# Weight preparation and two heads in a written-out order on every engine, in a Conformer block's forward and backward kernel

## The chip, the cores and the metric

The kernel runs on one core of one Trainium2 chip. The metric is the device time of one execution in microseconds (us); lower is better. Kernels are compared only within the same rounds. A profiled execution also gives a trace with every instruction's start and duration. "Span" is its time from the first to the last instruction.

The engines are called as in the profile: PE is TensorE's matmul, PEld its weight load, DVE is VectorE, ACT is ScalarE, POOL is GpSimd, SP is SyncE, which issues DMAs here. SPq and ACTq are the DMA issues of SP and of ACT.

## The reference

Two batches of 4000 tokens, 144 channels, bfloat16. One layer norm feeds an attention of one head and a gated convolution path; the reference returns the output and the gradients of `x` and all seven weights.

```python
xa  = _layernorm(x)
q, k, v = split(xa @ w_qkv)
p   = softmax(q @ k.T * D ** -0.5)                 # 4000 x 4000 per batch
glob = (p @ v) @ w_att_out
u, g = split(gelu(xa @ w_mlp_in))
gc  = depthwise_conv(_layernorm(g), dw_csgu)       # 5 taps
loc = (u * gc) @ w_mlp_out
m   = concat(glob, loc)
out = x + (m + depthwise_conv(m, dw_merge)) @ w_merge
# returned: out and the vjp for grad_out with respect to x and the 7 weights
```

## The kernel before

The program works on batch 0 and then batch 1, each in three stages: a **head**, the **attention** (32 row blocks of scores, forward and backward at once) and a **tail**. Only the heads are changed. A head turns `x` and `grad_out` into what the attention needs, in eight groups of 512 tokens. Its parts for a group g:

- normalisation (batch 0 alone; batch 1's is done earlier): `stats` on DVE, `power` on POOL, `nm` on DVE, then `apply`, shared among ACT, DVE and POOL;
- `stT` transposes the normalised `x` on PE, with copies out of PSUM on ACT and DVE;
- `stA` transposes `grad_out`; its last 16 channels are first packed for five taps by a POOL instruction (the group "g" in the profile, "narrow" below), and the copies out go to ACT and DVE;
- `stB(n)` multiplies, for two blocks of 128 tokens at a time: `pq` (the scores' left side Q) and `pb` (the gradient with the taps folded into the weights, in `GL`), and copies them out to `Q_t` and `B_t` on ACT and to `dug` on DVE. The head does the first eight of sixteen such steps; the rest run inside the attention.

Batch 0's head also prepares the weights: `M1` (the product of the q and k weights), the tap-scaled products `GL`, and others that are needed only later. `Weights.first` stands ahead of the groups, `Weights.second` behind them. A list scheduler orders the instructions on each engine from the program; the programmer's order is a priority, not an order of execution.

```python
def turn(self, src, R, c0, C, name, ps, pool=None):      # a weight, transposed
    ...
    if C % 128:
        nc.vector.memset(t[:, nck - 1, :], 0.0)
    for cc in range(nck):
        for kt in range(nk):
            ...
            pt = ps.tile([128, 128], BF, tag="tp", name="pt")
            nc.tensor.transpose(pt[0:w, 0:rk], src[...], self.W.ident[0:rk, 0:rk])
            nc.vector.tensor_copy(t[0:w, cc, kt * 128:kt * 128 + rk], pt[0:w, 0:rk])

def first(self, ps, then):
    ... # loads, then() = loads of x and of grad_out's first three groups, transposes, M1
    for h in range(2):
        ...
        for kt in range(2):
            for kk in range(5):
                if h == 0:
                    nc.vector.tensor_scalar(A[:, kt, 4 - kk, :], UT[h][:, kt, :], W.wm[:, h, kt, kk:kk + 1], None, op0=ALU.mult)
                else:
                    nc.gpsimd.tensor_scalar(A[:, kt, 4 - kk, :], UT[h][:, kt, :], W.wm[:, h, kt, kk:kk + 1], 1.0, op0=ALU.mult, op1=ALU.mult)
                nc.gpsimd.tensor_scalar(Bz[:, kt, 4 - kk, :], Wmh[:, h, kt, 128:D], W.wm[:, h, kt, kk:kk + 1], 1.0, op0=ALU.mult, op1=ALU.mult)
        ... # products of Wmh with A and of Bz with UT into GL, GL80

def apply(self, g):
    nc.vector.scalar_tensor_tensor(nm[:], mv[:, :, 0], -1.0, rs, op0=ALU.mult, op1=ALU.mult)
    for j in range(4):
        if self.b or j % 2 == 0:
            nc.scalar.activation(self.S.xaa[:, g * 4 + j, :], xg[:, j, :], ACT.Identity, bias=nm[:, j:j + 1], scale=rs[:, j:j + 1])
        else:
            (nc.vector if j == 1 else nc.gpsimd).tensor_scalar(...)

# phase_head:
for s in range(NGR + 2):
    if s < NGR:
        stA(s)                       # in batch 0 with stats, power, apply of group s
    if 0 <= s - 1 < NGR:
        stT(s - 1)
    if s == NGR:                     # 16 rows of R into the attention's operand
        nc.sync.dma_start(S.R_d[:], R[112:128, :])
        ... # 8 copies (batch 1) or 4 (batch 0), "row copies" below
    if 0 <= s - 2 < NGR:
        stB(s - 2, ...)
    if s == 5:
        ... # QB, jt0: the operand of the first score row
if wts:
    wts.second(ps_t, ps_2)
```

## Time and profile before

| | before |
|---|---|
| time, three runs | 1294.88 us (1293.71 to 1295.97) |
| span of the profiled execution | 1288.0 us (this execution's time was 1289.89 us, some 5 us under the median of these three) |
| first `pb` of batch 0 | 32.25 us |
| first score matmul (`pS`) of batch 0 / of batch 1 | 63.74 / 680.18 us |
| first `y` (second product of the attention) of batch 0 / of batch 1 | 95.91 / 708.97 us |

The page of the profile, parts 1 and 4: busy time (share of the span) and number of instructions of each engine, then how the chain of work that ended last divides among the engines.

```profile
PE 1211.8 (94%) x15116; PEld 949.9 (74%) x15116; DVE 962.3 (75%) x3293; ACT 843.5 (65%) x2498; POOL 558.8 (43%) x1033
...
PE 71%; DVE 13%; DMA 4%; issue 4%; ACT 4%; POOL 3%; SPq 1%; ACTq 0%; DVEq 0%; POOLq 0%
```

PE is busy for 94% of the span, so most of the kernel is bound by matmuls; but these are the attention and the tails. The heads look different. The next table gives the busy time of each engine in stretches of 3 us of before's head of batch 0 (columns: stretch, its length, then busy us and instructions of PE, PEld, DVE, ACT and POOL, the granted clock of PE, the share of DMA, GB/s; before's trace has no record of the clock ahead of 31.57 us, and the view prints 1.00 there).

```profile
19.00:22.00 3.00, 1.02 (x3) 0.28 (x3) 1.76 (x10) 0.89 (x2) 3.00 (x10) 1.00 0.68 240
22.00:25.00 3.00, 0.00 (x0) 0.00 (x0) 0.00 (x0) 0.00 (x0) 3.00 (x12) 1.00 0.00 0
25.00:28.00 3.00, 0.43 (x4) 0.44 (x5) 0.00 (x0) 0.00 (x0) 3.00 (x12) 1.00 0.00 0
28.00:31.00 3.00, 2.87 (x17) 1.96 (x16) 1.78 (x8) 1.06 (x3) 1.00 (x7) 1.00 0.71 246
```

From 22 to 28 us POOL works almost alone. The chain of waits of before names the work (columns: start, us, what):

```profile
26.83 0.25 POOL w_Bz L1224
27.08 0.44 POOL g L1428
27.57 0.65 PE pr L1431 x4
```

It is the end of a run of 30 small tap-scaled copies on POOL (ten of `w_A` and twenty of `w_Bz`, begun at 18.06 us; ten more of `w_A` are on DVE), then the packing of `grad_out`, then PE. The view of waits sums, from 9 to 60 us, the idle time of each engine by the instruction that waited and the one that released it (columns: who waited <- for whom: us in total, times, longest).

```profile
DVE nm L1383 <- POOL rstdx L1376: 9.6, 7, 4.0
...
DVE w_GL L1230 <- PE fw L1229: 8.5, 2, 8.0
...
PE pr L1431 <- POOL g L1428: 8.4, 3, 7.0
ACT ra L1386 <- DVE nm L1383: 8.3, 8, 4.3
```

PE and DVE wait for POOL and its results. Once `GL` stands, before's eight steps of `stB` in the head follow within 24.1 us (the first `pq` at 32.0 us, the eighth at 56.1).

### The profile page before, as it was taken

The numbers are of one execution on the slowest core, as the hardware profiler recorded it, in microseconds if no ns is written. First come the engines' busy times: TensorE is split into PE (matmuls) and PEld (weight loads), VectorE is DVE, ScalarE is ACT, GpSimd is POOL, SyncE is SP. The second block draws the span as 40 slices with busy tenths as digits, with TensorE's granted clock in tenths as the row PEclk, the third lists the DMA queues.
The fourth block names the chain that finished last, engine by engine and source line by source line (L and its number), as shares of the span: only waits on it lengthen the run. The fifth ranks groups of instructions, "written<-read, shape, count | busy, mean of one in ns | idle before, by whom it ended". The sixth has DMA issues, their size and how long they took to land.

```text
span 1288.0 us, 39900 instructions
## 1 busy us (share of the span) xinstructions
PE 1211.8 (94%) x15116; PEld 949.9 (74%) x15116; DVE 962.3 (75%) x3293; ACT 843.5 (65%) x2498; POOL 558.8 (43%) x1033
## 2 busy tenths in 40 slices
PE   4899999999999999998989999999999999998996
PEld 2657777777777777788975777777777777778994
DVE  4656778888888788857735677888878878885674
ACT  2667777767767766546646767777777767664542
POOL 6412444545444453257611244444544445324650
PEclk9999999999999999999999999999999999999998
DMA  6378989898989989887775889899888999987861
GB/s 185 88 142 147 156 155 159 155 167 151 161 151 159 170 155 165 151 190 216 202 220 109 152 156 152 153 169 170 148 160 153 154 170 155 164 154 182 238 168 29
DMA packets 634223, 205.51 MB, mean 160 GB/s; under 512 B 577183, under 2 KB 631556, under 8 KB 633988
## 3 DMA queue, kind: packets, MB, share of 16 engines
q1 hardware_dynamic: 627472, 197.54, 80.6%
q10 hardware_dynamic: 6548, 5.33, 1.7%
q8 instruction: 120, 1.97, 0.6%
q14 instruction: 83, 0.68, 0.2%
HBM read 46.22 MB, written 21.79 MB: 53 GB/s over the span
## 4 chain that ended last, share of the span: by engine, by line
PE 71%; DVE 13%; DMA 4%; issue 4%; ACT 4%; POOL 3%; SPq 1%; ACTq 0%; DVEq 0%; POOLq 0%
PE y L1911 15%; PE pS L1865 9%; PE X L1933 9%; PE X L1934 8%; PE pD L1865 7%; PE pS L1861 5%; DVE Sm L1875 5%; PE pc L1573 3%; PE pb L1467 2%; PE po L2088 2%; PE EF L2063 1%; DVE jg L1792 1%; PE gr L2159 1%; DVE acc L1949 1%; ACT Qs L1894 1%
## 5 line engine op out<-in xcount | busy, mean ns | idle before, releaser
L1875 DVE SCALAR_TENSOR_TENSOR Sm<-pD,Pm 128x500 bf16<-128x500 f32 x512 | 325.7, 673 | 80.3 <-PE pD L1865 47.6
L1873 ACT ACTIVATE Pm<-pS 128x500 bf16<-128x500 f32 x512 | 295.5, 586 | 41.2 <-PE pS L1865 38.3
L1933 PE MATMUL X<-Qs,Sm 128*128 128x144 bf16 x2048 | 285.6, 226 | 9.3 <-DVE acc L1949 8.9
L1946 POOL TENSOR_TENSOR acc<-xs,acc 128x432 f32<-128x432 f32 x150 | 168.5, 1123 | 280.5 <-ACT xs L1945 280.0
L1934 PE MATMUL X<-Bt,Pm 128*128 128x144 bf16 x2048 | 285.4, 226 | 0.7 <-DVE Bt L1898 0.7
L1934 PEld LDWEIGHTS <-Pm 128*128 128x128 bf16 x2048 | 199.9, 98 | 11.9 <-issue 11.3
L1933 PEld LDWEIGHTS <-Sm 128*128 128x128 bf16 x2048 | 199.8, 98 | 1.5 <-issue 0.9
L1911 PEld LDWEIGHTS <-PT 128*128 128x128 bf16 x2048 | 136.5, 97 | 30.7 <-issue 2.4
L1911 PEld LDWEIGHTS <-ST 128*128 128x128 bf16 x2048 | 136.4, 97 | 27.6
L1945 ACT COPY xs<-X 128x432 f32<-128x432 f32 x150 | 77.9, 519 | 111.4 <-PE X L1934 103.4
L1949 DVE TENSOR_TENSOR acc<-X,acc 128x432 f32<-128x432 f32 x180 | 104.0, 578 | 53.9 <-PE X L1934 53.2
L1873 ACT ACTIVATION_READ_ACCUMULATOR Pm<-pS 128x1 f32 x512 | 105.0, 205 | 0.0
L1861 PE MATMUL pD<-rb,QBr 16*128 16x500 bf16 x448 | 96.0, 378 | 3.3 <-DVE Sm L1875 2.8
L1865 PEld LDWEIGHTS <-BTm 128*128 128x128 bf16 x512 | 49.8, 98 | 59.9 <-issue 1.6
L1861 PE MATMUL pS<-rb,QBr 16*128 16x500 bf16 x448 | 91.9, 380 | 0.1
L1792 DVE SCALAR_TENSOR_TENSOR jg<-gnC,dgC 128x256 bf16<-128x256 bf16 x160 | 89.6, 560 | 1.0
L1921 POOL TENSOR_TENSOR B_t<-zd,yd 128x144 bf16<-128x144 f32 x64 | 34.0, 531 | 113.0 <-ACT zd L1920 112.7
L1865 PEld LDWEIGHTS <-QTm 128*128 128x128 bf16 x512 | 29.1, 97 | 72.5 <-issue 72.5
L1865 PE MATMUL pS<-rb,QTm 128*128 128x500 bf16 x256 | 76.9, 382 | 0.0
L1865 PE MATMUL pS<-ra,QTm 128*128 128x500 bf16 x256 | 76.5, 381 | 0.0
L1911 PE MATMUL y<-rb,PT 128*128 128x144 bf16 x1024 | 74.3, 226 | 1.0 <-ACT zd L1920 1.0
L1911 PE MATMUL y<-ra,PT 128*128 128x144 bf16 x1024 | 74.3, 226 | 1.1 <-ACT zd L1920 1.1
(626 smaller groups left out, 2895.0 us busy)
## 6 DMA issues: line engine op xcount, KB each, us to landing
gs<-in_grad_out_dram SPq DMA_DIRECT2D x24, 720.0 KB
dh_d<-dh SPq DMA_DIRECT2D x32, 144.0 KB
dhr<-dh_d SPq DMA_DIRECT2D x16, 288.0 KB
gs<-in_grad_out_dram SPq DMA_DIRECT2D x8, 540.0 KB
xg<-in_x_dram SPq DMA_DIRECT2D x21, 144.0 KB
dug_d<-dug SPq DMA_DIRECT2D x16, 144.0 KB
dug<-dug_d SPq DMA_DIRECT2D x32, 72.0 KB
ug_d<-ug SPq DMA_DIRECT2D x32, 72.0 KB
```

What stands on the lines that cost most here:

```text
L1573: nc.tensor.matmul(pc[:, q, 0:128], t[:, q * 128 + m:q * 128 + m + 128], W.dg[:, (4 - m) if back else m, :], start=(m == 0), stop=(m == 4))
L1792: nc.vector.scalar_tensor_tensor(jg[:], a_[:, m:m + 256], 1.0, d_[:, 2:258], op0=ALU.mult, op1=ALU.mult, accum_out=dws[:, p, m:m + 1])
L1861: nc.tensor.matmul(o_[h][:, 0:SC], jt[i // 4][2][rr, i % 4, :], S.XR[c2][rr, 0:SC], start=True, stop=False)
L1865: nc.tensor.matmul(o_[h][:, 0:SC], jt[i // 4][w][:, i % 4, :], S.xaT[:, c0:c0 + SC], start=False, stop=True)
L1873: nc.scalar.activation(P[:, pb, c1:c1 + SC], o_[h][:, 0:SC], ACT.Exp, accum_out=ld8[:, 0, n_:n_ + 1])
L1875: nc.vector.scalar_tensor_tensor(Sm[:, pb, c1:c1 + SC], o_[h][:, 0:SC], 1.0, P[:, pb, c1:c1 + SC], op0=ALU.mult, op1=ALU.mult, accum_out=l ...
L1911: nc.tensor.matmul(y[:, w, :], src[:, jj, :], S.xaa[:, j, :], start=(j == 0), stop=(j == NBK - 1))
L1933: nc.tensor.matmul(X[:, jj, :], Sm[:, i % NP, j * 128:(j + 1) * 128], Qs[:, i % 4, :], start=(kk == 0 and jj == 0), stop=False, skip_group ...
L1934: nc.tensor.matmul(X[:, jj, :], P[:, i % NP, j * 128:(j + 1) * 128], Bt[:, i % 4, :], start=False, stop=(kk == 1), skip_group_check=True)
L1945: nc.scalar.copy(xs[:, 0:nj, :], X[:, 0:nj, :])
L1946: nc.gpsimd.tensor_tensor(a_, xs[:, 0:nj, :], a_, op=ALU.add)
L1949: nc.vector.tensor_tensor(a_, X[:, 0:nj, :], a_, op=ALU.add)
```

## The change

The intent: prepare the weights earlier and with fewer instructions, share the work among DVE, POOL and ACT, and write out by hand the order of every engine, so that weight work that is needed later fills the gaps between the groups rather than stand behind them. In particular:

1. transposes of one weight share one PSUM bank and two copies; the zero fills of the transposed weights go to POOL;
2. the 40 scaled copies (30 on POOL, 10 on DVE) become four 720-wide products (two on DVE, two on POOL) and four 80-wide ones on DVE;
3. `second` becomes a generator `rest`, of which one portion runs after each group; `G` takes three copies per half; its weight stores go to ACT's queue; `apply` of both odd blocks of a group (j = 1 and 3) goes to POOL;
4. both heads stand in a `manual_schedule` block: each engine executes its instructions in exactly the order of the program.

The core of the diff:

```diff
 def turn(...):
         if C % 128:
-            nc.vector.memset(t[:, nck - 1, :], 0.0)
+            nc.gpsimd.memset(t[:, nck - 1, :], 0.0)
+        pt = ps.tile([128, nck, R], BF, tag="tp", name="pt")
         for cc in range(nck):
             for kt in range(nk):
-                pt = ps.tile([128, 128], BF, tag="tp", name="pt")
-                nc.tensor.transpose(pt[0:w, 0:rk], ...)
-                nc.vector.tensor_copy(t[0:w, cc, kt * 128:kt * 128 + rk], pt[0:w, 0:rk])
+                nc.tensor.transpose(pt[0:w, cc, kt * 128:kt * 128 + rk], ...)
+        n1 = C // 128
+        nc.vector.tensor_copy(t[:, 0:n1, :], pt[:, 0:n1, :])
+        if C % 128:
+            nc.vector.tensor_copy(t[0:C % 128, n1, :], pt[0:C % 128, n1, :])
 ... (40 copies out)
+    def taps(self):
+        for kt in range(2):
+            nc.vector.tensor_tensor(self.A[0][:, kt], self.UT[0][:, kt, :].unsqueeze(1).to_broadcast([128, 5, D]),
+                                    self.wr[:, 0, kt, :].unsqueeze(2).to_broadcast([128, 5, D]), op=ALU.mult)
+        ... # four products Bz, 80 wide, on DVE
+    def taps1(self, kt):
+        self.k.nc.gpsimd.tensor_tensor(self.A[1][:, kt], ...)          # 720 wide
 ... (second -> rest, with yields; memsets, dg, c80, WIM copies to gpsimd)
-            nc.sync.dma_start(W.fin[name][0][:], t[:])
+            nc.scalar.dma_start(W.fin[name][0][:], t[:])
 ... (apply)
-                (nc.vector if j == 1 else nc.gpsimd).tensor_scalar(...)
+                nc.gpsimd.tensor_scalar(...)
 ... (phase_head)
-        for s in range(NGR + 2):
-            ...
-        if wts:
-            wts.second(ps_t, ps_2)
+        with tc.manual_schedule():
+            ...
+            if wts:
+                wts.heads(ps_t, ps_2)
+                nrm.stats(0)
+                nrm.power(0)
+                wts.taps()
+                wts.taps1(0)
+                nrm.apply(0)
+                narrow(0)
+                wts.taps1(1)
+                wts.keys(ps_t, ps_2)           # w_qT, w_kT and M1
+                nrm.stats(1)
+                ...
+                rest = wts.rest(ps_t, ps_2)
+            ...
+            for n in range(-1, NGR):
+                if wts and 0 <= n + 4 < NGR and n >= -1:
+                    nrm.stats(n + 4)
+                    nrm.power(n + 4)
+                if 2 <= n + 3 < NGR:
+                    if wts:
+                        nrm.apply(n + 3)
+                    narrow(n + 3)
+                if n >= 0:
+                    stB(n, *tiles())
+                if 1 <= n + 2 < NGR:
+                    stT(n + 2)
+                    stA(n + 2)
+                    ...
+                if n == 5:
+                    spread()                   # R_d and all row copies
+                if n == 3:
+                    jit()
+                if rest:
+                    next(rest, None)
```

## The prediction

> **What bounds it now.** The span is 1288.0 us (timed median 1294.88), PE busy 94%. The chain of waits is 71% PE, nearly all in attention and tails, which the change leaves alone. Only the two heads change. Batch 0's first score matmul (pS) starts at 63.8 us and its first y group at 96.1; batch 1's at 680.3 and 709.1. Batch 1's head needs no weights and takes 24.4 us from the release of its buffers (655.9); so of batch 0's 64 us roughly 9 are first loads, 24 head, 30 weights and waits.
>
> The chain of the first 70 us names these waits: PE's second group of transposes waits for grad_out until 9.3 us, with weight work queued behind it. From 18.1 to 27.1 GpSimd makes 30 small scaled copies (w_Bz 293 ns, w_A 381 ns); in the stretches 22-25 and 25-28 the others are almost idle. Then each group passes the GpSimd power (1.01 us) and DVE. From 58 to 65 weight leftovers run, and the granted clock is about 0.5 from 62.5 to 69.
>
> **What the change does.**
> 1. Weight products come ahead of grad_out: PE and DVE can work from about 3 us. Gain 4 us.
> 2. The 30 copies become two 720-wide GpSimd products and DVE products. From GpSimd's two-input products (531 ns at 144 wide, 800 at 288, 1123 at 432) I estimate 1.7 us each: 3.5 us for 9.3. Gain 6 us.
> 3. Transposes share one bank and two copies instead of four; G takes three copies per half instead of six: some 40 fewer DVE/ACT instructions of 0.15-0.3 us. Leftovers are spread between groups, so most of 58-65 vanishes. Gain 3-5 us.
> 4. Costs: GpSimd takes memsets, diagonals, WIM copies and all odd normalisations, in order: the second product stands behind the narrowing of grad_out, the w_q/w_k memsets behind that. Adding up its list with the trace's durations, M1 is ready about 15 us, first pb about 20 (now 32.3), and the eighth narrowing ends about 43. Seven zero stores (0.45 us of issue each) move ahead of part of the first grad_out load. Cost about 3 us.
>
> So first pS comes at about 50 us, and GpSimd, not PE, paces batch 0's head. [...]
>
> Batch 1: same operations; PE paces it (2.8 us a group, about 2.6 of it matmul issue). The row copies into the attention operand now all issue after the last transposed group, where some went earlier. Gain 0-2 us.
>
> Clock: [...] the trace shows 0.50 at 64-68. Without the leftovers there, another 1-2 us.
>
> **Sum.** 14 (batch 0) + 1 (batch 1) + 1 (clock) = 16 us, all on the critical path, since attention cannot start earlier: **1279 us, range 1269 to 1288** (8 in 10). Faster by over 2%: 0.11; within 2%: 0.87; slower: 0.02.
>
> **What would show it.** First pS of batch 0 at 45-55 us, first pb near 20; no stretch over 3 us with GpSimd alone busy; GpSimd nearly full from 12 to 43. Batch 1 from release to first pS in 23-25 us. Attention and tails unchanged to 2 us.
>
> **What would make it wrong.** GpSimd slower than estimated, so that the order blocks PE behind it; grad_out landing late behind tiny loads on the queue; half clock through the head; batch 1's scores waiting for row copies. Or all waits go and pS comes near 40: over 20 us saved.

The 1-2 us for the clock are the estimate from the 0.50 in before's trace; that the clock would rise without the leftovers was not shown.

## The result and the profile after

Ratios here and below are the mean time of one kernel's fast runs over the mean of the other's fast runs of the same rounds, so they are not quite the ratio of the medians quoted beside them. Values below 1 mean faster than before.

| | before | after |
|---|---|---|
| time, median of four runs each | 1294.3 us (1291.9 to 1295.97) | 1296.85 us (1295.13 to 1298.43) |
| ratio to before, 95% interval | | 1.0021 (1.0000 to 1.0042) |
| span of the profiled execution | 1288.0 us | 1294.6 us |
| first `pb` of batch 0 | 32.25 us | 26.43 us |
| first `pS` of batch 0 / of batch 1 | 63.74 / 680.18 us | 66.83 / 682.58 us |
| first `y` of batch 0 / of batch 1 | 95.91 / 708.97 us | 96.81 / 713.51 us |

The predicted 1279 us (1269 to 1288) was missed: no gain showed, in place of 16 us. Of the 6.6 us between the two spans, some 4 are before's lucky execution; the timed medians differ by 2.6 us.

```profile
PE 1212.3 (94%) x15116; PEld 951.6 (74%) x15116; DVE 957.4 (74%) x3236; ACT 843.4 (65%) x2494; POOL 562.3 (43%) x1032
...
PE 71%; DVE 13%; DMA 4%; issue 4%; ACT 4%; POOL 1%; SPq 1%; ACTq 0%; DVEq 0%; POOLq 0%
```

PE's busy time is the same to 0.5 us. In the chain, POOL's share fell from 3% to 1%, so the 30 copies did leave it, but the span did not shrink with it.

Where the difference arises can be read from the attention. Its 32 rows in each batch start with one ACT instruction each; in after it starts 0.9 us later than in before in every row of batch 0, and 4.5 us later in every row of batch 1. Each attention therefore takes the same time, 463.0 us from its first such instruction to its last in both kernels. Of the 6.6 us between the spans, 0.9 arise ahead of batch 0's rows and 3.6 between the two batches' rows, where batch 0's tail and batch 1's head lie. The last 2.1 us lie behind the last row: the last tail took 130.1 us in after and 128.1 in before. No run changes the tail, and over the fourteen profiles it took 127.8 to 132.2 us, so these 2.1 us are within its spread. What counts is the chain ahead of the first row of each batch.

**Batch 0.** The first `pb` comes 5.8 us earlier, the first `pS` 3.1 us later. In between, after's eight steps of `stB` take 39.1 us (`pq` from 25.9 to 65.0 us) where before took 24.1. The view of waits of after, for the same stretch:

```profile
ACT ra L1415 <- DVE nm L1412: 12.0, 5, 5.6
...
PE fw L1151 <- DVE w_kT L1141: 8.1, 1, 8.1
PE tp L1457 <- ACT rb L1466: 7.6, 3, 3.3
POOL ve L1404 <- DVE nm L1412: 6.9, 4, 3.1
...
DVE go80f L1460 <- PE tp L1457: 5.0, 4, 2.2
...
ACT ra L1415 <- DMA wf_U<-w_l_s: 3.3, 1, 3.3
```

Now every engine waits for another: ACT for DVE, PE for ACT and DVE, DVE for PE, POOL for DVE. Here are six single microseconds of after (columns as in the stretches above):

```profile
34.00:35.00 1.00, 0.96 (x11) 0.59 (x9) 0.65 (x4) 0.00 (x0) 0.47 (x3) 1.00 0.89 318
35.00:36.00 1.00, 0.41 (x5) 0.31 (x5) 0.90 (x5) 0.00 (x0) 0.00 (x0) 1.00 0.34 125
36.00:37.00 1.00, 0.00 (x0) 0.00 (x0) 0.97 (x6) 0.28 (x1) 0.23 (x2) 1.00 0.00 0
37.00:38.00 1.00, 0.00 (x0) 0.00 (x0) 0.07 (x1) 1.00 (x5) 1.00 (x2) 1.00 0.04 15
38.00:39.00 1.00, 0.20 (x4) 0.20 (x4) 0.00 (x0) 1.00 (x4) 0.92 (x3) 1.00 0.83 199
39.00:40.00 1.00, 0.90 (x9) 0.42 (x6) 0.42 (x1) 0.72 (x2) 0.70 (x2) 0.57 0.72 215
```

In 36-37 DVE works nearly alone, in 37-38 ACT and POOL, and PE has almost nothing for 3 us. The instructions behind it, from the timeline of each engine of after (columns: start, us, engine, line, operation, output<-input, and in brackets the idle time before it and what ended it). DVE:

```profile
34.35 0.22 DVE L1143 COPY w_oT<-pt 16x144 bf16<-16x144 bf16 x1 [2.36 <-POOL w_oT L1133]
...
36.10 0.28 DVE L1396 BATCH_NORM_STATS2 st<-Sm 128x6 f32<-128x144 bf16 x1
...
36.51 0.13 DVE L1412 SCALAR_TENSOR_TENSOR nm<-mv,rstdx 128x4 f32<-128x4 f32 x1
...
39.22 0.42 DVE L1460 COPY go80f<-tp 80x512 bf16<-80x512 bf16 x1 [2.15 <-PE tp L1457]
```

ACT:

```profile
36.72 0.91 ACT L1415 ACTIVATE ra<-Sm,nm,rstdx 128x144 bf16<-128x144 bf16 x2 [5.54 <-issue]
37.53 0.37 ACT L1487 CAST Q_t<-pq 128x288 bf16<-128x288 f32 x1
...
38.15 0.60 ACT L1466 COPY rb<-pm 128x512 bf16<-128x512 bf16 x1
```

PE:

```profile
32.46 0.24 PE L1485 MATMUL pq<-w_M,rb 128*128 128x144 bf16 x1
...
38.80 0.38 PE L1457 MATMUL tp<-w_ident,g 128*80 128x128 bf16 x4 [3.35 <-ACT rb L1466]
```

Read them as one round. DVE's next instruction is the second copy of `w_oT`, a weight needed much later. It waits 2.36 us for a zero fill that stands on POOL behind `power`, two `apply` and a packing, and these behind POOL's own weight work from 26.87 to 31.3 us. Behind it on DVE stand eight statistics instructions of group 5 (one of them is shown), and only then `nm` of group 4, at 36.51 us. ACT's list has `apply` of group 4 next, so ACT stands idle for 5.54 us until 36.72 (the trace calls the wait's end "issue"; `nm`, which it reads, had ended at 36.64), though the matmuls of `Q_t` had started at 32.46. The copy `rb` out of PSUM stands behind that; PE's next transposes need the buffer that `rb` empties, and start at 38.80 (3.35 us idle); DVE's `go80f` waits for those. The next `pq` and `pb`, at 41.27 and 41.72, then stand on PE behind a portion of weight work (twelve matmuls from 39.29 us), although the last copy that `pq` needs had ended at 39.24. So `Q_t` starts 5.1 us after the first of its matmuls (37.53 against 32.46), behind an instruction that it doesn't need. Here, in the written order, the programmer had decided what is next, and an instruction that wasn't ready stopped what stood behind it: `apply` of group 4 held ACT's list for 5.54 us, the copy of `w_oT` DVE's for 2.36.

One more such wait is at the beginning: PE is idle from 8.3 to 16.44 us, before the product `M1`. From the timelines of DVE and POOL of after:

```profile
11.58 1.35 DVE L1412 SCALAR_TENSOR_TENSOR nm<-mv,rstdx 128x4 f32<-128x4 f32 x1 [0.31 <-POOL rstdx L1405]
...
16.03 0.22 DVE L1143 COPY w_qT<-pt 16x144 bf16<-16x144 bf16 x1 [2.95 <-POOL w_qT L1133]
```

```profile
11.53 1.38 POOL L1239 TENSOR_TENSOR w_A<-w_lT,w_wr 128x720 bf16<-128x720 bf16 x1
...
14.45 1.39 POOL L1239 TENSOR_TENSOR w_A<-w_lT,w_wr 128x720 bf16<-128x720 bf16 x1
15.78 0.22 POOL L1133 MEMSET w_qT<- 128x144 bf16 x1
```

The second copy of `w_qT` waited 2.95 us for a fill of 0.22 us, which stood on POOL behind `taps1(1)`, which had stood behind `apply(0)` and `narrow(0)`. The `nm` at 11.58 us took 1.35 us, beside POOL's 720-wide product, and ended at 12.93 as the product did (12.91); the median of after's sixteen `nm` is 0.15 us. POOL's `ve` and `power` took 0.75 and 1.56 us at 9.15 and 9.98 us, next to DVE's products of 720 and 80 columns; their medians are 0.19 and 1.02. No run tested these overlaps by themselves.

**The clock.** Every stretch at half rate (granted clock 0.50) that the traces of before and of after record in the two heads lasts 3.41 us or 6.83. But their records of the clock begin only at 31.57 us in before and at 22.08 us in after, and the views print 1.00 where there is none. What the clock was there can be read from one and the same group of matmuls earlier and later, from the timelines of PE of before and of after:

```profile
18.26 0.61 PE L1425 MATMUL pm<-w_ident,gs 128*128 128x128 bf16 x4
...
50.27 0.39 PE L1425 MATMUL pm<-w_ident,gs 128*128 128x128 bf16 x4
```

```profile
17.75 0.63 PE L1452 MATMUL tp<-w_ident,gs 128*128 128x128 bf16 x4
...
22.22 0.39 PE L1452 MATMUL tp<-w_ident,gs 128*128 128x128 bf16 x4
```

The starts of neighbouring transposes lie 107 ns apart ahead of the first record and 55 behind it (medians, both traces), so in these groups ahead of the first record PE ran at half rate; that it did so from the start is an estimate from them. When full rate comes these two traces do not settle: it came 5.6 us into a stretch in which PE was hardly idle in after (from 16.44 us) and 4.0 us into one in before (from 27.57), and an earlier one in before, from 11.58 to 20.56 us with PE busy for 7.9 of its 9.0 us in mostly small matmuls, did not bring it. After came to full rate 9.5 us sooner than before, and fell back to half in 25.50-28.91, 39.15-45.98 and 52.80-56.22 us, before in 62.29-69.12. The first two falls of after come near the end of a wait of PE (2.96 us up to 25.57, 3.35 up to 38.80). At half rate the five `pb` matmuls at 41.72 us took 1.41 us, where the five at 32.25 us in before took 0.78. Adding up half of the time at half rate from 0 to 75 us, with half rate up to the first record, after lost 17.9 us of full clock and before 19.2; by the records alone it is 6.8 and 3.4. The clock therefore does not explain by itself why after is not faster; r3_all4g, below, says more.

**Batch 1** has no weight work, and it still lost. From the timeline of SP, before and after: the row copies and the load `Rz`, of which the first score row's `ph` makes use.

```profile
668.78 1.38 SPq L1485 DMA_DIRECT2D rb<-Sm  x2
...
677.67 1.15 SPq L1485 DMA_DIRECT2D ra<-Sm  x2
...
681.06 0.83 SPq L1669 DMA_DIRECT2D Rz<-R_d  x2
```

```profile
679.16 0.72 SPq L1506 DMA_DIRECT2D rb<-Sm  x1
...
683.80 0.59 SPq L1506 DMA_DIRECT2D ra<-Sm  x1
...
685.11 0.84 SPq L1746 DMA_DIRECT2D Rz<-R_d  x2
```

In before, six of the eight copies had gone by 676.5 us. In after all eight were issued in one piece from 679.16 to 684.4 us, about 0.6 us each, and `Rz` stood behind them; PE waited 1.09 us for a row copy at 684.06 us and 0.52 us for `Rz` at 687.32. The first `pS` came 2.4 us later than in before. From the head's `go80f`, the first copy of packed and transposed `grad_out`, which waits for a buffer in both kernels, to the first `pS` it took 25.7 us in after (656.91 to 682.58) and 24.3 in before (655.89 to 680.18). In that stretch of after PE waited six times some 0.3 us, 1.8 in all, for DVE's copy `Sm`, a wait that before's list does not have. From the first `pS` to the first `y`, where the row copies and `Rz` are waited for, it took 30.9 us against 28.8.

### The profile page after: what moved, and what is told of

It is laid out like the page before. It is cut to its first block, busy times and chain, and to the rows that moved or that the text cites. A ratio compares the mean times of both kernels' runs of the same rounds, so it can differ in the third digit from the quotient of the medians.

```text
span 1294.6 us, 39840 instructions
## 1 busy us (share of the span) xinstructions
PE 1212.3 (94%) x15116; PEld 951.6 (74%) x15116; DVE 957.4 (74%) x3236; ACT 843.4 (65%) x2494; POOL 562.3 (43%) x1032
## 4 chain that ended last, share of the span: by engine, by line
PE 71%; DVE 13%; DMA 4%; issue 4%; ACT 4%; POOL 1%; SPq 1%; ACTq 0%; DVEq 0%; POOLq 0%
PE y L1988 15%; PE pS L1942 9%; PE X L2010 9%; PE X L2011 8%; PE pD L1942 7%; PE pS L1938 5%; DVE Sm L1952 5%; PE pc L1650 2%; PE pb L1493 2%; PE po L2165 2%; PE EF L2140 2%; DVE jg L1869 1%; PE gr L2236 1%; DMA y<-r 1%; DVE acc L2026 1%
## 5 line engine op out<-in xcount | busy, mean ns | idle before, releaser
L2011 PEld LDWEIGHTS <-Pm 128*128 128x128 bf16 x2048 | 200.2, 98 | 11.9 <-issue 11.3
```

Source lines behind the costliest of these rows:

```text
L2011: nc.tensor.matmul(X[:, jj, :], P[:, i % NP, j * 128:(j + 1) * 128], Bt[:, i % 4, :], start=False, stop=(kk == 1), skip_group_check=True)
```

## Experiments

Two accounts stood against each other.

- **Order**: the operations are good, but the fixed lists of the engines wait for each other in a ring. With the same operations in the scheduler's order the predicted gain should appear, and repairs of single places in the order should each give a part.
- **GpSimd too slow** (the prediction's own claim): POOL got so much work that it paces the head; then adding POOL work must delay the head by as much, and removing the order must do little.

A third, that the wide copies themselves are costly, had to be excluded too. (The expectations call the first two theories A and B; C is the half clock, D the issue of batch 1's row copies.) The columns of the following table: time (median) and ratio to before with 95% interval; first `pS` of batch 0; offset of the score rows against before's profile in batch 0 and in batch 1 (us, median of 32 rows, negative is earlier). Offsets compare one profile with one. The three kernels with the same code for batch 0 (after, r1_rows, r3_b1auto) show 0.9, 3.7 and -0.9 us there, so a single offset is good to some 2 us, and all of them share before's lucky execution.

| run | time (us) | ratio | first `pS` | rows b0 | rows b1 |
|---|---|---|---|---|---|
| before | 1292.95 to 1295.13 | 1 | 63.74 | 0 | 0 |
| after | 1296.85 | 1.0021 (1.0000 to 1.0042) | 66.83 | +0.9 | +4.5 |
| r1_auto | 1285.29 | 0.9937 (0.9919 to 0.9956) | 54.05 | -9.1 | -8.0 |
| r1_swap | 1296.41 | 1.0022 (1.0004 to 1.0039) | 63.80 | -2.0 | +3.2 |
| r1_fills | 1297.05 | 1.0019 (1.0002 to 1.0035) | 63.32 | -3.0 | +5.4 |
| r1_rows | 1296.64 | 1.0010 (0.9993 to 1.0028) | 67.91 | +3.7 | +7.7 |
| r2_wide | 1288.67 | 0.9963 (0.9946 to 0.9979) | 57.24 | -2.7 | -0.8 |
| r2_poolend | 1303.17 (two runs) | 1.0079 (1.0059 to 1.0100) | 70.18 | +3.9 | +9.5 |
| r2_stores | 1297.85 | 1.0047 (1.0029 to 1.0065) | 66.17 | +4.6 | +7.6 |
| r2_all4 | 1288.91 | 0.9966 (0.9943 to 0.9990) | 59.52 | -1.8 | -0.3 |
| r3_b1auto | 1295.20 | 1.0008 (0.9986 to 1.0031) | 65.21 | -0.9 | -1.2 |
| r3_all3 | 1290.64 | 0.9964 (0.9942 to 0.9986) | 61.49 | -4.7 | -0.7 |
| r3_all4g | 1285.39 | 0.9935 (0.9912 to 0.9958) | 58.69 | -7.5 | -5.1 |
| r3_auto80 | 1282.03 | 0.9911 (0.9885 to 0.9937) | 53.31 | -11.8 | -11.3 |

The medians of before in the rounds of r1, r2 and r3 were 1294.17, 1292.95 and 1295.13 us. All runs gave correct results. By the rule of 2% every ratio in the table is "same"; what is said of gains below rests on the intervals and on the profiles.

### r1_auto: the same operations, without the written order

```diff
-        with tc.manual_schedule():
+        if True:
```

> The changed kernel with its hand-made order taken away in both heads (the scheduler places the same instructions, same engines, same wide copies). In the changed kernel batch 0's first pS starts at 66.8 us and the first y at 97.0, and batch 1 needs 56.8 us from buffer release (656.9) to the first y (713.7); before: 63.8, 96.1 and 53.2. Theory A (the fixed order makes the engines wait for each other in a ring): first pS of batch 0 at 54 to 60 us, batch 1 back to 53 to 54 us, total 5 to 10 us below the changed kernel. Theory B (GpSimd has too much work, whatever the order): first pS stays at 64 or later. Theory C [...]: first pS moves only if the clock does.

Measured: 1285.29 us against 1294.17, and first `pS` at 54.05 us, 12.8 us earlier than after with the same instructions (as many on each engine). From the timelines of PE, the first `pS` of after and of this run:

```profile
66.83 0.38 PE L1938 MATMUL pS<-rb,QBr 16*128 16x500 bf16 x1
```

```profile
54.05 0.38 PE L1938 MATMUL pS<-rb,QBr 16*128 16x500 bf16 x1
```

The same stretch of waits as above, of this run:

```profile
ACT ra L1415 <- DVE nm L1412: 9.4, 7, 4.0
...
PE fw L1151 <- DVE w_kT L1141: 4.3, 1, 4.3
...
DVE go80f L1460 <- PE tp L1457: 2.8, 2, 1.9
```

PE's wait for `rb` is gone from the list (7.6 us in after), `M1` waits 4.3 us in place of 8.1, and `go80f` 2.8 in place of 5.0. From 0 to 60 us PE is busy 43.78 us here and 37.64 in after. So the operations in the scheduler's order give 8.9 us, somewhat over half of the 16 predicted, and the written order takes them away: this is the experiment that decides between the two accounts, and it decides for the order.

### r1_swap: one exchange within the written order

`apply` and packing of group n+3 go ahead of the statistics of group n+4, so that `nm` no longer stands behind eight instructions which nobody waits for.

```diff
-                if wts and 0 <= n + 4 < NGR and n >= -1:
-                    nrm.stats(n + 4)
-                    nrm.power(n + 4)
                 if 2 <= n + 3 < NGR:
                     ...
                     narrow(n + 3)
+                if wts and 0 <= n + 4 < NGR and n >= -1:
+                    nrm.stats(n + 4)
+                    nrm.power(n + 4)
```

> The changed kernel with one pair exchanged in the group loop of batch 0: a group's normalisation is issued ahead of the statistics of the group after it. The work is the same on each engine. Theory A: the ring DVE statistics, normaliser, ScalarE normalisation, ScalarE copies, PE transposes, DVE copy loses the 1.7 us of statistics; groups come every 4.2 to 4.8 us in place of 5.9 and first pS falls from 66.8 to 58 to 62 us; total 4 to 8 us lower. Theory B (GpSimd throughput) and theory C (clock): no change beyond 1.5 us. Batch 1 unchanged in all.

Measured: first `pS` 3.0 us earlier than in after and the rows of batch 0 2.9 us earlier, but the time is unchanged: 1296.41 us. In the profile batch 1 fell back by 5.2 us against batch 0 (in after by 3.6). A miss in the time, and in the first `pS` too (63.80 us, where 58 to 62 was expected); the part that was aimed at did move.

### r1_fills: the zero fills on DVE, early

```diff
 def turn(...):
-        t = (pool or self.tmp).tile([128, nck, R], BF, name=name)
-        if C % 128:
-            nc.gpsimd.memset(t[:, nck - 1, :], 0.0)
+        t = self.early[name]          # allocated and zeroed with nc.vector.memset in loads()
 (the same for w_qTz and w_mT)
```

> The changed kernel with eight zero fills of weight tiles moved from GpSimd, where they stand in line behind normalisation work, to VectorE in the first microseconds. Theory A: the two waits of VectorE for these fills (2.95 us before the first w_q copy, 2.36 us before the w_o copy) go; M1 products start near 13.5 in place of 16.4 us, first pS 3 to 5 us earlier. Theory B: GpSimd saves about 2 us of work, so first pS about 2 us earlier, not more. Batch 1 unchanged.

Measured: `M1` starts at 13.25 us, as expected, first `pb` at 23.51 us (2.9 earlier), first `pS` 3.5 us earlier, rows of batch 0 3.9 us earlier than in after. The time stayed at 1297.05 us, a miss; in the profile batch 1 fell back by 8.4 us.

### r1_rows: batch 1's row copies in two parts

```diff
-        def spread():
-            nc.sync.dma_start(S.R_d[:], R[112:128, :])
+        def spread(part):
+            if part:
+                nc.sync.dma_start(S.R_d[:], R[112:128, :])
+            XRw = (S.XRw if part else []) if b == 0 else S.XRw[part:part + 1]
 ...
                 if n == 5:
-                    spread()
+                    spread(1)
                 if n == 3:
+                    spread(0)
                     jit()
```

> The changed kernel with batch 1's row copies into the attention operand issued in two parts: four after the group that completes the first 3000 tokens, four at the end, in place of all eight at the end. Theory D (batch 1 lost its time to the issue of copies on one queue, 0.6 us each, and the loads queued behind them): release to first y of batch 1 falls from 56.8 to 53 to 54.5 us, total 2 to 4 us lower. If batch 1's loss lies in the order of the compute engines, it stays at 56 to 57. Batch 0 unchanged.

Measured: 1296.64 us. The profile is of the slowest of the five executions (1301.68 us); in it batch 1 still added 4.0 us to its offset, and the granted clock was at half from 659.8 to 666.6 us (in after from 657.0 to 660.4). Alone this repair shows no gain, a miss. Over all profiles the growth from batch 0 to batch 1 was 3.0 to 8.4 us in the five written-order kernels without it (after 3.6, r1_swap 5.2, r1_fills 8.4, r2_poolend 5.6, r2_stores 3.0), and 4.0, 1.5, 4.0 and 2.4 us in the four with it (r1_rows, r2_all4, r3_all3, r3_all4g).

### r2_wide: the wide copies alone, on the kernel before

```diff
 (before) turn: one PSUM bank, two copies, as in the change
+        for m in range(5):
+            nc.gpsimd.tensor_copy(wr[:, :, :, m], W.wm[:, :, :, 4 - m])
 ...
-                for kk in range(5):
-                    ... (40 scaled copies)
+                (nc.gpsimd if h else nc.vector).tensor_tensor(A[:, kt], ...)      # 720 wide
+                nc.vector.tensor_tensor(Bz[:, kt], ...)                           # 80 wide
```

> The kernel before with only the arithmetic made wider: each turned weight goes through one PSUM bank and two copies in place of four, the 30 scaled copies become products (four of 720 columns and four of 80). Order left to the scheduler, everything else as before. Theory A (the widening is worth what was predicted, and the fixed order gave it back): the stretch from 18 to 27 us with GpSimd alone shrinks by 5 us or more, first y of batch 0 at 86 to 91 (before 96.1), total 5 to 9 us below before, so most of the 8.9 us that the changed kernel without its fixed order gained. If the gain of that kernel came from the moved engines and the earlier loads instead, this one gains less than 3 us.

Measured: 1288.67 us against 1292.95, and first `pS` 6.5 us earlier than in before. This was step 2 of the prediction with part of step 3; the wide operations are good in themselves, and the account that they cost too much falls. But 4.3 us is less than the 5 to 9 expected, and only 2.7 us of the 6.5 remain at the score rows in this profile. So widening makes about half of r1_auto's 8.9 us; what makes the other half (earlier loads, moved engines, the portions of `rest`) was not tested.

### r2_poolend: more work for POOL

Four fills of no use, 128x512 each, at the end of each of five groups.

```diff
                 if rest:
                     next(rest, None)
+                if wts and n < 4:
+                    for _ in range(4):
+                        nc.gpsimd.memset(idle[:], 0.0)
```

> The changed kernel with useless work on GpSimd: four fills of 128x512 (0.52 us each, 2.1 us in all) at the end of each of five groups of batch 0, where nothing waits for them. Theory B (GpSimd throughput sets the pace, as predicted): every group comes 2.1 us later, first pS 10 us later, about 77. Theory A ([...] GpSimd has 2 to 3 us idle in a group): first pS within 3 us of 66.8.

```profile
41.92 2.27 POOL L1580 MEMSET idle<- 128x512 bf16 x4
45.03 0.19 POOL L1404 TENSOR_SCALAR ve<-mv 128x4 f32<-128x4 f32 x1 [0.84 <-DVE nm L1412]
```

Five times 2.27 us is 11.4 us of POOL work, put between the groups. First `pS` came at 70.18 us, 3.4 later than in after (2.3 to 5.0 later than in the three profiles with after's code for batch 0); had POOL paced the whole head, it would have come near 77. The second line shows why: even with this addition POOL then waits 0.84 us for DVE. POOL had slack, and the rival falls as an account of the whole head. The eight packings `g` on POOL show where the delay arises. Against after the first three end at the same time, the next three 2.2 to 2.3 us later, the last two 3.2 and 3.1. So the first four fills, at 31.25 us, arrived in full: there, from 24.15 to 34.5 us, POOL works through weights and normalisation with no pause over 0.23 us in after, and does set the pace. The fourth set cost 1.0 us, the others nothing. The time rose by more, some 7.5 us by the two ratios (two runs); the profile has 3.0 of that at batch 0's rows, and the rest is not explained.

### r2_stores: the seven weight stores on SP

In after ACT issues seven stores from 53.53 to 57.11 us (0.36 to 0.77 us each), and `apply` of a group stands behind them (the line with "DMA" in after's waits, 3.3 us).

```diff
-            nc.scalar.dma_start(W.fin[name][0][:], t[:])
 ... (the loop moved to the end of rest())
+            nc.sync.dma_start(W.fin[name][0][:], t[:])
```

> The changed kernel with the seven stores of prepared weights moved from ScalarE's queue, amid the groups, to SP's queue at the end of the head. Theory A: ScalarE loses the 53.5 to 57.2 us stretch in which it issues stores and a normalisation waits behind them; first pS 2 to 4 us earlier (63 to 65), total 1 to 4 us lower. Theories B and C: no change beyond 1.5 us at first pS.

Measured: no gain, a miss: 1297.85 us, ratio 1.0047 (after: 1.0021, the intervals overlap). First `pS` came 0.7 us earlier, but the rows of batch 0 3.7 us later than in after. On SP the seven stores stood from 67.01 to 70.3 us ahead of the first attention row's `Rz` load, which in after was issued at 67.73 and here at 70.63. So on SP too the stores stood ahead of something urgent: `Rz` was issued 2.9 us later.

### r2_all4: four repairs together

`r1_swap`, `r1_fills`, `r1_rows` and `r2_stores` in one kernel, still in the written order.

> The changed kernel with four repairs of its order together: the exchange of statistics and normalisation, the early zero fills, the row copies of batch 1 in two parts, the stores at the end. Work per engine is that of the changed kernel. Single repairs moved the first y of batch 0 by 3 to 4 us each and the total not clearly. Theory A: taken together the ring is cut in several places at once: first pS of batch 0 at 50 to 56 us, first y at 80 to 86, total 1281 to 1288 us, near the scheduler's order. If instead another resource sets the pace, first pS stays above 60.

Measured: 1288.91 us against 1292.95, ratio 0.9966; first `pS` 7.3 us earlier than in after. Four repairs, none of which gained time alone, gained together: against before 0.9966 where after has 1.0021, about 7 us. Taken away alone, a wait left the time to the others (ratios 1.0010 to 1.0047). The size was missed: first `pS` at 59.52 us, where 50 to 56 was expected.

### r3_all3: the same without moving the stores

> Three repairs of the changed order (exchange, early fills, row copies in two parts), stores left where they were on ScalarE's queue. With the stores on SP's queue at the end of the head the four repairs gave first pS at 59.5 us but first y only at 93.7, and the stores alone there gave 100.3: the stores held up SP's loads and transposes in the first attention row. Theory A: first pS at 56 to 61, first y 27 to 31 us after it (85 to 91); total 1283 to 1289 us. If the stores on SP were not the reason, the gap stays at 34 us.

Measured: 1290.64 us, ratio 0.9964; the stores on SP (r2_all4) and on ACT (here) give the same time. The first `y` follows 29.6 us after the first `pS`, where it was 34.2 with the stores on SP, as expected; but the first `pS` came 2.0 us later, and the time lies 1.6 us above the expected range.

### r3_all4g: the four repairs with the stores on POOL's queue

```diff
-            nc.scalar.dma_start(W.fin[name][0][:], t[:])
 ... (the loop moved to the end of rest())
+            nc.gpsimd.dma_start(W.fin[name][0][:], t[:])
```

> The four repairs with the stores at the end of the head on GpSimd's queue, which is idle there. Theory A: ScalarE has no stores amid the groups and SP none either: first pS at 53 to 58, gap to first y 28 to 31 us, total 1280 to 1287 us.

Measured: 1285.39 us, ratio 0.9935, as good as the scheduler's order with after's operations. First `pS` at 58.69 us (53 to 58 was expected), rows of batch 0 at -7.5. In the same rounds the four runs of r3_all3, which differs only in the place and the queue of the stores, took 1288.55 to 1293.13 us, and these took 1284.46 to 1287.87. POOL had little left to do at that point: it issues the stores from 49.50 to 53.5 us, fills two tiles, and is then idle for 12.8 us.

This run also bears on the clock: by the records PE was at half rate from 21.45 to 35.10 us, a loss of 6.8 us as in after, and yet the first `pS` came 8.1 us earlier than in after.

### r3_b1auto: batch 0 in the written order, batch 1 in the scheduler's

```diff
-        with tc.manual_schedule():
+        with tc.manual_schedule() if b == 0 else ExitStack():
```

> The changed kernel with the fixed order taken away in batch 1's head only. Batch 1 lost 3.6 us against before in the profile of the changed kernel (offset of its rows 4.5 us, of batch 0's rows 0.9). Theory A and D (the fixed order, with all row copies at its end, made batch 1's loss): the offset grows by 0 to 1.5 us from batch 0 to batch 1 in place of 3.6, total 1 to 4 us below the changed kernel. If the loss came from the tail or from the clock alone, it stays at 3 to 4 us.

Measured: the row offset went from -0.9 in batch 0 to -1.2 in batch 1. The growth of 3.6 us of after is gone, which speaks for the written order as the cause of batch 1's loss too, in one profile (of the fastest of the four executions, 1291.48 us). The time, 1295.20 us against 1295.13, cannot separate this from after (ratio 1.0008 against 1.0021, in other rounds and with wide intervals).

### r3_auto80: scheduler's order, early fills, and a late weight moved back

`r1_auto` with the fills of `r1_fills`, and with `w80f` (a copy on DVE that reads tiny loads) and the block that makes `c80` (affine selects on POOL, wanted only later) at the end of `rest` rather than at its start.

```diff
-        w80f = tp_.tile([128, 2], F32, name="w_w80f")
-        ... (its copy on DVE)
-        i80 = tp_.tile([128, DR], BF, name="w_i80")
-        ... (affine selects, c80)
 ... (end of rest)
+        w80f = tp_.tile([128, 2], F32, name="w_w80f")
+        ... (its copy on DVE)
+        i80 = tp_.tile([128, DR], BF, name="w_i80")
+        ... (affine selects, c80)
```

> The scheduler's order (as the first run of the series, total 1285.3) with the early zero fills, and with the uses of ten tiny weight loads moved to the end of the weights: in that run the VectorE waited until 27.4 us for these loads, which leave their queue only at 21 to 25 us, with statistics behind. Theory A: that wait goes, first pS 2 to 5 us earlier than 54.1, first y at 82 to 86, total 1280 to 1285 us. If the wait was harmless: no change beyond 1.5 us.

Measured: 1282.03 us against 1295.13, ratio 0.9911 (0.9885 to 0.9937), first `pS` at 53.31 us; over the first 60 us PE is busy 45.04 us where it was 36.98 in before and 37.64 in after. This is the lowest time of all runs. Against r1_auto the gain is not shown: the intervals overlap, and the first `pS` came 0.7 us earlier where 2 to 5 was expected. Nor does r1_auto's trace have the wait that the expectation names: there `w80f` was copied at 36.7 us with no idle time of DVE before it, and here at 37.5.

## Why the prediction was wrong

**What bounds it (right).** Attention and tails, PE-bound, were not touched: every one of the 32 score rows of a batch carries the same offset. Of the 6.6 us between the spans 4.5 arise ahead of the rows; the 2.1 behind them are within the spread of the tail.

**Steps 1 to 3, the gains of 4, 6 and 3-5 us (right in mechanism, too high in the sum).** With the operations of the change in the scheduler's order (r1_auto) the first `pS` of batch 0 moved from 63.74 to 54.05 us, that is 9.7 us. The prediction's own terms for batch 0 give 4 + 6 + 4 - 3 = 11 us; its sum of 14 left the cost of step 4 out; the wide copies with one-bank transposes alone (r2_wide) gave 6.5 at the first `pS`, against 6 predicted for step 2, but 4.3 in time. Steps 1 and 3 were not tested one by one. POOL's product, estimated at 1.7 us, took 1.38; the run of 30 copies with POOL alone is gone. The prediction cited a factor between the two engines for two tensor inputs; the trace of before had one input, `w_A`, at 381 ns on POOL and 239 on DVE, a factor of 1.6. After has an operation with two, the 720-wide product, and it took 1.38 and 1.39 us on POOL and 0.88 and 0.90 on DVE, again a factor of some 1.6.

**Step 4 and its conclusion (wrong): "So first pS comes at about 50 us, and GpSimd, not PE, paces batch 0's head."** This is the step that failed. It added up the list of one engine, with durations from the trace, and read the end of that list as the end of the head. As time that was wrong: the prediction had POOL nearly full from 12 to 43 us, when the eighth packing (its "narrowing") would end; POOL was busy for 20.3 of those 31 us, and the packing ended at 55.6. It waited for DVE's statistics (6.9 us in one group of waits, which the view puts down to the `nm` right behind them), DVE for PE's transposes and POOL's fills, PE for ACT's copies, ACT for DVE's `nm`. In after's first 60 us no engine stood out: PE was busy 37.64 us, POOL 36.10, DVE 30.76 and ACT 26.04. First `pS` came at 66.83 us, not 50; `M1` at 16.44 and first `pb` at 26.43, not 15 and 20. What the groups cost in this written order is the length of the ring through all four engines (39.1 us for the eight steps of `stB`), not the longest of the four lists. The runs put a number to both: without the order 12.8 us back at the first `pS` (r1_auto); 11.4 us of added POOL work cost 3.4, of which 2.2 at the one place, near 31 us, where POOL did set the pace (r2_poolend). The prediction's list of what could be wrong had "the order blocks PE behind it" only for a POOL slower than estimated. POOL was not slower in the product, and the order blocked all the same.

**Batch 1, "Gain 0-2 us" (wrong).** The profile shows a loss of 3.6 us there; with the scheduler's order in that head alone (r3_b1auto) the growth was -0.3 us, so the cause is in all likelihood the same. The row copies that the prediction named as a danger are a part. With the copies split, the growth from batch 0 to batch 1 was 3.0 us in the mean of four profiles, against 5.2 over five without; with batch 1 in the scheduler's order (r1_auto, r2_wide, r3_b1auto, r3_auto80: 1.1, 1.9, -0.3 and 0.5) it was 0.8. In the trace of after 1.4 us of the loss lie ahead of the first `pS`, in the rhythm of the groups, and 2.1 behind it, where the row copies and `Rz` are waited for; neither part was tested clear of noise.

**Clock, "another 1-2 us" (an estimate, not shown).** The half clock left the stretch at 60-69 us, as predicted, and came back between 25 and 60 us: by the records 6.8 us of clock lost in place of 3.4, with the half rate ahead of the first record 17.9 in place of 19.2. What the clock alone is worth was not tested. By itself it cannot be what the miss comes from: r3_all4g lost 6.8 us by the records too, and gained.

**The sum.** Predicted 16 us; measured between the medians -2.6 us. The operations themselves, in the scheduler's order, gave 8.9 us (1294.17 to 1285.29), and the order took them back. Repairing four places in the order gave them again (r3_all4g: 9.7 us between the medians).

## What to carry to other kernels

When a change fixes the order on every engine, walk one round of the loop through all the engines' lists and look for what stands ahead of the instruction the next engine waits for; the sum of one engine's list is only a lower bound (here 43 us for the eighth packing, which ended at 55.6). Work that is not urgent (weights for later, fills, stores) belongs behind the urgent work of each group, on a queue where nobody waits (r3_all4g, stores at the end on POOL's queue, 1285.39 us; r3_all3, amid the groups on ACT's, 1290.64), and a single repair may show nothing until the next place in the ring is repaired as well (alone 1.0010 to 1.0047 of before's time, the four together 0.9966, r2_all4). Before hand-ordering, run the same operations in the scheduler's order: here that one line was worth more than the whole written order (11.6 us between the medians of after and of r1_auto, from different rounds; 0.84% by the two ratios, about 11 us).
